# Routed experts with at most 32 tokens: from a block of 128 rows each to four column groups of one shared block

## The chip, the cores and the metric

The kernel runs on one core of one Trainium2 chip. The metric is the device time of one execution in microseconds, taken as the median of the runs of a kernel. The core has five engines with queues of their own: PE (TensorE, matrix products into PSUM; the weight loads are listed as PEld), DVE (VectorE), ACT (ScalarE), POOL (GpSimd) and SP, which here only issues DMA transfers. Each works through its own instructions in order and waits on semaphores for the others.

## The reference

Three stages follow one another: attention with rotary embedding, a sparse mixture of experts (each token goes to one of 8 experts), and a dense one (each token goes through all 8). The change is in the second:

```
logits = xn @ en.T / tau                      # 1152 tokens, 8 experts
expert_idx = np.argmax(logits, axis=1)
gate_w = probs[np.arange(N), expert_idx]
for e in range(E):
    mask = expert_idx == e
    h = np.maximum(x[mask] @ w1[e], 0.0)      # 512 -> 1024
    out[mask] = gate_w[mask, None] * (h @ w2[e])   # 1024 -> 512
```

How many tokens an expert gets is known only when the kernel runs. Worked out on the host from the reference with the inputs it draws, the eight experts get 83, 414, 6, 601, 17, 3, 28 and 0 tokens.

## The kernel before, in words

After attention, `route_half` finds each token's expert, its rank among that expert's tokens, and its place in a list of blocks; a block has 128 rows (`BLK`) of one expert, and an expert takes as many blocks as its tokens need, so 1 + 4 + 1 + 5 + 1 + 1 + 1 + 0 = 14 here. `place` turns the places into an index list per block with small bf16 products on PE, `blocks` writes the expert of each block into `bei`, from which SP loads registers. `NS` blocks (14) are always run, unrolled; a part under `tc.If` (two more blocks) runs only if there are more than `NS`.

One pass of the loop in `run_blocks` is a step `i`, and its instructions are issued in the order in which they are written (a manual schedule fixes it for PE, DVE, ACT and POOL). A step has, on PE: the first layer of block i (`block_l1`, 24 products of 128x512), the transposes of block i+1's tokens (`block_x`), the second layer of block i-1 (`block_l2`, 24 products), and the transposes of block i's hidden layer (`block_turn`). Every fp32 operand is split into a high and a low part of a faster type (fp32r) and three products are summed, so for each block ACT makes a rounded copy of the weights (`whi`, four pieces, L682) and DVE the rest (`wlo`, four pieces, L675). SP fetches the weights of a block only if its expert differs from the block's before. POOL gathers a block's tokens (L690) and scatters its output (L747) by indirect DMA. PSUM has eight banks: four for the first layer (two tiles `h`), two `x` for all transposes and index products, two `y` for the second layer.

At step 1 `place_rest` places the gate values and the scatter indices. In steps 7 to 12 the generator `dense` prepares the first weights of the third stage, whose tiles `w` are a ring of eight in the pool `early`. The third stage (`dense_experts`) follows the blocks; its `sinkhorn` computes routing logits with products of 32 columns in four column groups side by side (L1092), in plain fp32.

Of the kernel before, what the change touches and what calls it, by code (L numbers as in the profile page):

```python
# [25 lines left out]
QT = 120  # L26
TW = [120, 120, 120, 120, 96]
NQ = 5
BLK = 128
NB = 16  # L30
NS = 14
# [9 lines left out]
for name_, width_ in (("u", 128), ("slot", 1), ("rev", E), ("revm", NQ * E), ("j", E * (E + 1)),  # L41
                      ("tri", E * E), ("iota", 128), ("idh", B * NQ), ("idl", B * NQ)):
    COLS[name_] = slice(C_END, C_END + width_)
    C_END += width_
# [3 lines left out]
def fused_kernel(ctx, tc, qk, vv, tab, cst, emb, tau, w1a, w2a, wg, w1b, w2b, out):  # L48
# [22 lines left out]
    gate = keep.tile([BLK, NB], F32, name="gate")  # L71
    idx = keep.tile([BLK, 2, NB], U32, name="idx")
    bei = keep.tile([1, NB + 1], I32, name="bei")
# [319 lines left out]
    mx, fi, rk = tmp("mx", [QT, B, NQ]), tmp("fi", [QT, NQ]), tmp("rk", [QT, NQ])  # L393
# [4 lines left out]
    t9, t8 = tmp("t9", [QT, E, E + 1]), tmp("t8", [QT, E, E])  # L398
    nb, st, en = (tmp(n, [QT, E]) for n in ("nb", "st", "en"))
# [3 lines left out]
    G.memset(ohb[:, :, NQ], 0.0)  # L403

    def route_half(b):
# [16 lines left out]
        if b > 0:  # L422
            V.tensor_tensor(t9, over(rp[:, NQ], 2, [QT, E, E + 1]), col("j", a=E), op=ALU.is_gt)
        yield V.tensor_tensor(w5, rp[:, :NQ], ohb[:, b, :NQ], op=ALU.mult)
        if b > 0:
            V.reduce_sum(out=nb, in_=t9, axis=AX.X)
        yield V.reduce_sum(out=rk, in_=w5, axis=AX.X)
        if b > 0:
            V.tensor_tensor(t8, over(nb, 1, [QT, E, E]), col("tri", a=E), op=ALU.mult)
        yield V.tensor_copy(ri_, rk)  # L430
        if b > 0:
            V.reduce_sum(out=st, in_=t8, axis=AX.X)
# [24 lines left out]
        V.tensor_copy(idx[:, 0], p[:, :NB])  # L457
# [10 lines left out]
    def blocks():  # L468

        be, lim, tx, sx = tmp("be", [1, NB]), tmp("lim", [1, NB]), tmp("tx", [1, NB, E]), [1, NB, E]  # L470
        V.tensor_tensor(en, st, nb, op=ALU.add)
        V.tensor_copy(bei[:, NB:], en[0:1, E - 1:E])
# [4 lines left out]
        V.tensor_copy(bei[:, :NB], be)  # L477

# [6 lines left out]
    gv = tmp("gv", [QT, 3, B, NQ, NB], BF16)  # L485

    def gates():
# [15 lines left out]
        for x in range(3):  # L503
            part = tmp(f"gp{x}", [QT, B * NQ], BF16)
# [7 lines left out]
    def place_rest(bank_):  # L512
# [3 lines left out]
        V.tensor_copy(gate, p[:, :NB])  # L516
# [3 lines left out]
        V.tensor_tensor(ig, idx[:, 0], ig, op=ALU.subtract)  # L520
        V.tensor_copy(idx[:, 1], ig)
# [182 lines left out]
    def block_l1(x, w):  # L704
        p = bank("h", 2, "h", (128, 2, 512))
# [49 lines left out]

    def run_blocks(lo, hi, xb=None, w1=None, w2=None):
# [11 lines left out]
        with tc.manual_schedule(engines=ORDERED):  # L768
# [10 lines left out]
            for i in range(lo, hi + 1):  # L779
                begin, here, more = i == 0, i < hi, i + 1 < hi  # L780

                if here:
                    p = block_l1(x, w1)
                if begin:
# [14 lines left out]
                if begin:  # L799
# [4 lines left out]
                    next(gated)  # L804
                if i + 2 < hi and len(xb) < i + 3 - lo:
# [10 lines left out]
                if i == 1:  # L816
                    place_rest(lambda: bank("x", 2, "gp"))
# [571 lines left out]
```

## Time and profile before

| | us |
|---|---|
| median of 3 runs (lowest, highest) | 1148.04 (1146.05, 1149.77) |
| the profiled execution, device time | 1145.97 |
| its span, first to last instruction | 1144.2 |
| first product of block 0's first layer | 183.9 |
| first transposes of the dense stage | 371.0 |

All times below are of the profiled execution, in us from the start of its span. A row of the timeline gives the start, the time taken, engine, line and operation, the tile written and the tiles read, and how many instructions were merged; the brackets hold the idle time before it and what ended it. Products overlap: the time taken of one is longer than the distance to the next.

### The profile page before, as it was taken

How to read it: one execution, taken by the hardware profiler on the slowest of the kernel's cores; microseconds unless marked ns; L12 is line 12 of the kernel's file. 1: busy time of each engine (PE TensorE's matmuls, PEld its weight loads, DVE VectorE, ACT ScalarE, POOL GpSimd, SP SyncE). 2: the span in 40 equal slices, each digit the busy share in tenths (PEclk: the TensorE clock that was granted, in tenths of full speed). 3: DMA queues.
4: the chain of work that ended last, by engine and by line, in shares of the span. 5: the costliest groups of instructions: out<-in, count | busy, mean ns of one | idle time of the engine just before them, and what ended most of it. 6: DMA issues, size and time to landing. Idle time of an engine off the chain costs nothing.

```text
span 1144.2 us, 17210 instructions
## 1 busy us (share of the span) xinstructions
PE 1120.3 (98%) x6696; PEld 963.3 (84%) x6696; DVE 814.8 (71%) x1262; ACT 507.5 (44%) x772; POOL 145.2 (13%) x109
## 2 busy tenths in 40 slices
PE   8999997999999999999999999999999999999998
PEld 4677775888887998898998899899999899989997
DVE  6767769888884588776667767676667666676665
ACT  4656646888883453333333323333333323332330
POOL 7664402234321000000000000000000000000000
PEclk9999998999999999999999999999999999999999
DMA  8688614273495311111112211111111111111002
GB/s 249 171 238 248 169 32 142 92 256 120 157 340 166 94 38 38 47 47 55 38 38 56 56 38 37 39 55 56 38 38 56 47 46 38 38 56 56 19 1 83
DMA packets 75459, 103.64 MB, mean 91 GB/s; under 512 B 5224, under 2 KB 46696, under 8 KB 74608
## 3 DMA queue, kind: packets, MB, share of 16 engines
q1 hardware_dynamic: 72528, 94.12, 26.8%
q0 software_dynamic: 2240, 7.34, 1.9%
q8 instruction: 53, 0.87, 0.3%
q10 hardware_dynamic: 608, 1.07, 0.2%
q14 instruction: 30, 0.25, 0.1%
HBM read 111.09 MB, written 8.39 MB: 104 GB/s over the span
## 4 chain that ended last, share of the span: by engine, by line
PE 66%; DVE 1%; DMA 1%; issue 0%; POOLq 0%; SPq 0%
PE o L1202 34%; PE d L1148 28%; PE d L1165 2%; DMA g<-yd 0%; DMA yd<-y,idx 0%; DVE acc L1208 0%; PE d L1045 0%; PE o L1092 0%; PE d L1042 0%; DVE h L1190 0%; DVE w L915 0%; DVE w L977 0%; PE o L1045 0%; DVE acc L1213 0%; DVE P L1127 0%
## 5 line engine op out<-in xcount | busy, mean ns | idle before, releaser
L1202 PE MATMUL o<-w,h 128*128 128x512 f32 x1728 | 433.3, 393 | 0.4 <-DVE acc L1208 0.4
L1148 PEld LDWEIGHTS d<-yq,w 128*128 128x128 f32 x2520 | 355.8, 188 | 17.3
L1148 PE MATMUL d<-yq,w 128*128 128x288 f32 x2520 | 367.2, 294 | 0.0
L1202 PEld LDWEIGHTS o<-w,h 128*128 128x128 f32 x1728 | 312.2, 188 | 55.8 <-DVE acc L1208 0.7
L1213 DVE SCALAR_TENSOR_TENSOR acc<-o,P,acc 128x512 f32<-128x512 f32 x252 | 189.1, 750 | 159.0 <-PE o L1202 159.0
L1189 ACT ACTIVATE h<-st 128x576 fp32r<-128x576 f32 x90 | 61.9, 687 | 217.1 <-DVE st L1179 217.1
L1176 ACT ACTIVATE st<-d 128x576 f32<-128x576 f32 x90 | 58.7, 653 | 216.7 <-PE d L1148 216.7
L675 DVE TENSOR_TENSOR wlo<-raw,whi 128x2048 fp32r<-128x2048 f32 x56 | 127.9, 2288 | 17.2 <-ACT whi L682 17.2
L682 ACT ACTIVATE whi<-raw 128x2048 fp32r<-128x2048 f32 x52 | 99.8, 1919 | 9.7 <-DMA raw<-w1a 4.0
L1179 DVE TENSOR_TENSOR st<-st,d 128x576 f32<-128x576 f32 x90 | 67.6, 752 | 39.4 <-PE d L1148 39.4
L247 DVE TENSOR_REDUCE nb<-s 120x1 f32<-120x576 f32 (+1 forms) x80 | 60.3, 754 | 38.7 <-PE s L241 25.3
L253 ACT ACTIVATE p<-s,nb 120x576 f32<-120x576 f32 (+1 forms) x80 | 59.1, 739 | 48.1 <-DVE nb L247 45.8
L914 ACT ACTIVATE w<-raw 128x512 fp32r<-128x512 f32 x124 | 71.4, 576 | 19.8 <-DVE raw L960 16.2
L915 DVE TENSOR_TENSOR w<-raw,w 128x512 fp32r<-128x512 f32 x124 | 76.8, 620 | 0.0
L1190 DVE SCALAR_TENSOR_TENSOR h<-st,h 128x576 fp32r<-128x576 f32 x90 | 67.5, 750 | 0.4 <-ACT h L1189 0.3
L241 PE MATMUL s<-kd,qd 128*120 128x288 f32 x280 | 54.6, 317 | 2.5 <-ACT p L253 2.5
L241 PEld LDWEIGHTS s<-kd,qd 128*120 128x120 f32 x280 | 38.6, 178 | 15.2 <-ACT ph L279 5.7
L298 PE MATMUL o<-ph,vr 120*64 120x288 f32 x320 | 46.8, 417 | 0.0
L740 PE MATMUL y<-whi,hh 128*128 128x512 f32 x112 | 45.0, 402 | 0.0
L740 PE MATMUL y<-wlo,hh 128*128 128x512 f32 x112 | 42.9, 391 | 0.2 <-DVE wlo L675 0.2
L1190 DVE SCALAR_TENSOR_TENSOR h<-d,h 128x576 fp32r<-128x576 f32 x38 | 28.8, 757 | 19.3 <-ACT h L1189 19.3
L747 POOL DMA_INDIRECT yd<-y,idx x14 | 26.8, 1914 | 122.4 <-ACT y L746 97.3
(258 smaller groups left out, 1164.0 us busy)
## 6 DMA issues: line engine op xcount, KB each, us to landing
raw<-w1a SPq DMA_DIRECT2D x56, 512.0 KB
raw<-w2a SPq DMA_DIRECT2D x56, 512.0 KB
raw<-w1b SPq DMA_DIRECT2D x64, 256.0 KB
raw<-w2b SPq DMA_DIRECT2D x32, 512.0 KB
kd<-hl SPq DMA_DIRECT2D x28, 288.0 KB
r<-qk SPq DMA_DIRECT2D x6, 1152.0 KB
qd<-hl SPq DMA_DIRECT2D x28, 144.0 KB
g<-yd SPq DMA_DIRECT2D x4, 576.0 KB
```

What stands on the lines that cost most here:

```text
L241: T.matmul(s[:m, h, :HS], qd[:, j, t * QT:t * QT + m], kd[:, j, x, h * HS:(h + 1) * HS], start=(x == 0), stop=(x == 1))
L675: V.tensor_tensor(lo, raw, hi, op=ALU.subtract)
L682: A.activation(hi, raw, AF.Copy)
L740: T.matmul(p, h[a][:, k * 128:(k + 1) * 128], w[k // 2][b][:, (k % 2) * 512:(k % 2 + 1) * 512], start=(n == 0), stop=(n == len(todo) - 1))
L914: A.activation(hi, src, Copy)
L915: V.tensor_tensor(lo, src, hi, op=ALU.subtract)
L1148: T.matmul(d[1][:, q, :QW], wv[:, wx, which, k], yq[yx][:, YQ[p], k, q * QW:(q + 1) * QW], start=new and k == 0 and (wx, yx) == (0, 0), st ...
L1179: V.tensor_tensor(halves(st[x]), halves(st[x]), mid(d), op=ALU.add)
L1189: A.activation(hi, src, AF.Relu)
L1190: V.scalar_tensor_tensor(lo, src, 0.0, hi, op0=ALU.max, op1=ALU.subtract)
L1202: T.matmul(d, hs[n][:, r, hx, t * 128:(t + 1) * 128], w2[n][:, wx, r], start=(r == 0 and (hx, wx) == (0, 0)), stop=(r == 1 and hx == 1))
L1213: V.scalar_tensor_tensor(a, d, p, a, op0=ALU.mult, op1=ALU.add)
```

## The change

Experts with 1 to 32 tokens, the first four of them (all but expert 0), get no block. They share one further block ("quad") in which group g, rows 32 g to 32 g + 31, belongs to the g-th of them. `NS` becomes 10. The quad's products are plain fp32, without the split: 4 groups x 16 products of 128x32 weights against 128x512, one eighth (`quad_product(s)`, 8 products) at the end of the second layer in steps 2 to 8, the last in step 9. Its tokens are placed in step 1 (`place_quad`), gathered, transposed in step 2 (`quad_tokens`); its ReLU stands in step 5, its hidden layer's transposes in step 6 (`quad_turn`). Its weights are fetched in eight stages of four 512 KB transfers (`quad_fetch`) into the ring of `early`, which it now shares with the dense stage. The first layer has one `h` tile in PSUM where it had two; the two banks become `q`. The steps of `dense` move to 6, 7, 8, 8, 9, 9.

```
-NS = 14
+NS = 10
+NG = 4
+GS = BLK // NG
...
+    def before(dst, src):
+        V.tensor_tensor(t8, over(src, 1, [QT, E, E]), col("tri", a=E), op=ALU.mult)
+        V.reduce_sum(out=dst, in_=t8, axis=AX.X)
...  # in route_half, second half
+            V.tensor_tensor(few, t9[:, :, 0], t9[:, :, E + 1], op=ALU.subtract)
+            V.reduce_sum(out=nb, in_=t9[:, :, :E + 1], axis=AX.X)
+            before(grp, few)
...
+            V.scalar_tensor_tensor(inq, grp, NG - 0.5, few, op0=ALU.is_lt, op1=ALU.mult)
...
+            V.tensor_tensor(nb, nb, inq, op=ALU.subtract)
+            before(st, nb)
+            V.tensor_tensor(en, st, nb, op=ALU.add)
+            V.scalar_tensor_tensor(st, inq, float(NB), st, op0=ALU.mult, op1=ALU.add)
...  # blocks(): five more DVE operations for the experts of the quad
+    def place_quad(bank_):
+        z, qi = tmp("z", [QT, E]), tmp("qi", [BLK, 2])
+        V.tensor_scalar(z, grp, float(GS), 1024.0, op0=ALU.mult, op1=ALU.add)
+        V.scalar_tensor_tensor(z, inq, -1024.0, z, op0=ALU.mult, op1=ALU.add)
+        V.tensor_tensor(ws, ohb[:, :, :NQ], z..., op=ALU.mult)
+        V.tensor_reduce(blk, ws, axis=AX.X, op=ALU.add)
+        V.tensor_tensor(blk, blk, rk, op=ALU.add)
+        V.tensor_tensor(slot..., over(col("iota"), 1, sl), over(blk..., 2, sl), op=ALU.is_equal)
+        p = bank_()
+        for b in range(B):
+            for c in range(NQ):
+                T.matmul(p[:, :6], slot[:m, b, c], qv[:m, n], ...)
...  # then six small DVE operations: idx and gate of the quad
+    def quad_product(s):
+        for n in range(2):
+            k = s if s < KD_ else 2 * (s - KD_) + n
+            if s == 0 or (s, n) == (KD_, 0):
+                quad["p", n] = bank("q", 2, "q")
+            p = quad["p", n if s < KD_ else 0]
+            for g in range(NG):
+                own = slice(g * GS, (g + 1) * GS)
+                T.matmul(p[own], quad["x"][:, k * 128 + g * GS:k * 128 + (g + 1) * GS],
+                         quad["w", s][g][:, n * 512:(n + 1) * 512], ...)
...  # in run_blocks
                 if here:
                     p = block_l1(x, w1)
+                if lo == 0 and i == 2:
+                    quad_tokens()
+                elif lo == 0 and i == 6:
+                    quad_turn()
+                elif lo == 0 and i == 9:
+                    quad_product(7)
+                    block_out(NB, quad["p", 0])
...
                 if i == 1:
                     place_rest(lambda: bank("x", 2, "gp"))
+                    place_quad(lambda: bank("x", 2, "gp"))
+                    quad["xb"] = block_in(NB)
+                if lo == 0 and 2 <= i <= 8:
+                    quad_product(i - 2)
+                    if i == 5:
+                        quad_relu()
...
+                if lo == 0 and 1 <= i <= 7:
+                    quad_fetch(i)
```

DVE in the second half of the routing, from the counts of the experts (`t`, made from `rp`) to the first use of the block starts (`ws`). Before:

```order
L423 TENSOR_TENSOR t_131<-rp,cs 120x72
L424 TENSOR_TENSOR w_126<-rp,ohb 120x40
L426 TENSOR_REDUCE nb<-t_131 120x8
L427 TENSOR_REDUCE rk<-w_126 120x5
L429 TENSOR_TENSOR t_132<-nb,cs 120x64
L430 CAST ri__127<-rk 120x5
L432 TENSOR_REDUCE st<-t_132 120x8
L433 TENSOR_SCALAR rb__128<-ri__127 120x5
L434 TENSOR_SCALAR ri__127<-ri__127 120x5
L445 TENSOR_TENSOR ws<-ohb,st 120x80
```

Now, the first twelve of the seventeen up to `ws`:

```order
L429 TENSOR_TENSOR t_131<-rp,cs 120x80
L430 TENSOR_TENSOR w_126<-rp,ohb 120x40
L432 TENSOR_TENSOR few<-t_131 120x8
L433 TENSOR_REDUCE nb<-t_131 120x8
L408 TENSOR_TENSOR t_132<-few,cs 120x64
L409 TENSOR_REDUCE grp<-t_132 120x8
L435 TENSOR_REDUCE rk<-w_126 120x5
L437 SCALAR_TENSOR_TENSOR inq<-grp,few 120x8
L438 CAST ri__127<-rk 120x5
L440 TENSOR_TENSOR nb<-nb,inq 120x8
L408 TENSOR_TENSOR t_132<-nb,cs 120x64
L409 TENSOR_REDUCE st<-t_132 120x8
```

The expert counts now pass through `few` and `grp` before the block starts `st` exist.

DVE in step 1, where the index products end (`idx<-ig`) and the split of block 1's second-layer weights begins. Before, the split follows at once:

```order
L516 COPY gate<-gp 128x16
L519 TENSOR_SCALAR ig<-gp,cs 128x16
L520 TENSOR_TENSOR ig<-idx,ig 128x16
L521 CAST idx<-ig 128x16
L675 TENSOR_TENSOR wlo<-raw_79,whi 128x2048
```

Now there are six operations up to `slot`, then those that wait for PE's ten products with it (`gp`):

```order
L539 CAST idx<-ig 128x16
L549 TENSOR_SCALAR z<-grp 120x8
L550 SCALAR_TENSOR_TENSOR z<-inq,z 120x8
L551 TENSOR_TENSOR ws<-ohb,z 120x80
L552 TENSOR_REDUCE blk<-ws 120x10
L553 TENSOR_TENSOR blk<-blk,rk 120x10
L555 TENSOR_TENSOR slot<-cs,blk 120x1280
L562 TENSOR_REDUCE qi<-gp 128x1
L563 CAST idx<-qi 128x1
L564 TENSOR_REDUCE gate<-gp 128x1
L565 TENSOR_SCALAR qi<-gp,cs 128x1
L566 TENSOR_TENSOR qi<-qi 128x1
```

On PE the ten products stand between `place_rest` and the transposes of block 1's hidden layer.

ACT in the changed kernel, end of step 5 and start of step 6 (`xh` belongs to block 6's tokens, `raw_79` and `raw_80` are block 5's second-layer weights):

```order
L746 ACTIVATE xh<-xt 128x512
L844 ACTIVATE h<-q 128x512 x2
L728 ACTIVATE whi<-raw_79 128x2048
L792 ACTIVATE y<-y,gate 128x512
L728 ACTIVATE whi<-raw_80 128x2048
L773 ACTIVATE hh<-ht 128x512 x2
L852 ACTIVATE qh<-qht 128x512 x2
L728 ACTIVATE whi<-raw_77 128x2048
```

In the other steps `whi<-raw_79` follows `xh` directly; here the quad's ReLU, which waits for the quad's product behind the second layer, stands between.

## Rows read from the trace of the kernel before

**Rows 1.** The page, part 1: busy us, share of the span, instructions

```profile
PE 1120.3 (98%) x6696; PEld 963.3 (84%) x6696; DVE 814.8 (71%) x1262; ACT 507.5 (44%) x772; POOL 145.2 (13%) x109
```

**Rows 2.** Windows, four steps: stretch, length, busy us per engine, PE clock, DMA, GB/s

```profile
232.30:281.40 49.10, 49.10 (x242) 40.84 (x241) 43.07 (x29) 42.06 (x37) 17.61 (x8) 1.00 0.56 195
```

**Rows 3.** Timeline of PE, one step of the block loop, then the last

```profile
281.49 0.71 PE L710 MATMUL h<-whi,xh 128*128 128x512 f32 x2
...
287.06 0.60 PE L697 MATMUL xt<-io,xb 128*128 128x128 f32 x4
...
293.00 1.03 PE L725 MATMUL ht<-io,h 128*128 128x128 f32 x8
293.79 0.71 PE L710 MATMUL h<-whi,xh 128*128 128x512 f32 x2
...
343.36 0.66 PE L725 MATMUL ht<-io,h 128*128 128x128 f32 x4 [0.59 <-DVE xl L701]
```

**Rows 4.** L1092: the chain's piece, the line's products, timeline of PEld

```profile
384.21 2.75 PE o L1092 x35
...
L1092 PE MATMUL o<-yt,lw x52: 219/379/510, 384.1 to 386.6; 128*32 128x256 f32 x24, 128*32 128x64 f32 x12, 128*32 128x384 f32 x8, 128*32 128x192 f32 x8
...
384.14 1.10 PEld L1092 LDWEIGHTS o<-yt,lw 128*32 128x32 f32 x23 [0.16 <-issue]
...
386.88 1.22 PEld L1165 LDWEIGHTS d<-yq,w 128*128 128x128 f32 x9 [0.41 <-issue]
```

**Rows 5.** Timelines of DVE in the routing, and of PE in step 0

```profile
173.73 0.22 DVE L423 TENSOR_TENSOR t<-rp,cs 120x72 f32<-120x72 f32 x1
...
174.92 0.23 DVE L445 TENSOR_TENSOR ws<-ohb,st 120x80 f32<-120x80 bf16 x1
...
193.44 0.66 PE L725 MATMUL ht<-io,h 128*128 128x128 f32 x4 [1.08 <-DVE xl L701]
```

**Rows 6.** Timelines of PE and DVE in step 1, and line L438

```profile
205.33 0.91 PE L465 MATMUL gp<-gv,slot 120*128 120x16 bf16 x30
206.62 0.40 PE L465 MATMUL gp<-ib,slot 120*128 120x16 bf16 x10 [0.38 <-DVE xl L701]
...
207.53 0.17 DVE L521 CAST idx<-ig 128x16 uint32<-128x16 f32 x1
207.64 4.50 DVE L675 TENSOR_TENSOR wlo<-raw,whi 128x2048 fp32r<-128x2048 f32 x2
...
L438 DVE TENSOR_TENSOR slot<-cs,ri__127 x2: 811/816/820, 151.0 to 176.5; 120x640 bf16<-120x640 f32 x2
```

**Rows 7.** Windows around light stretches of PE, and PE's timeline

```profile
174.90:181.70 6.80, 4.55 (x28) 3.25 (x28) 5.96 (x18) 6.22 (x10) 2.51 (x2) 0.50 0.25 70
181.70:189.50 7.80, 7.13 (x32) 5.44 (x32) 7.31 (x17) 2.52 (x2) 5.29 (x3) 1.00 0.88 316
189.50:193.80 4.30, 1.62 (x12) 1.14 (x11) 3.91 (x9) 3.66 (x5) 0.00 (x0) 1.00 0.26 102
205.30:207.70 2.40, 2.02 (x48) 1.85 (x48) 1.92 (x7) 1.02 (x2) 0.00 (x0) 1.00 0.03 9
...
178.17 3.73 PE L754 MATMUL warm<-whi 128*128 128x512 f32 x8 [0.36 <-DVE en L471]
```

**Rows 8.** Timelines of PE, ACT and DVE from the end of step 2

```profile
219.24 1.03 PE L725 MATMUL ht<-io,h 128*128 128x128 f32 x8
...
219.43 0.69 ACT L746 ACTIVATE y<-y,gate 128x512 f32<-128x512 f32 x1 [0.80 <-PE y L740]
220.02 1.91 ACT L682 ACTIVATE whi<-raw 128x2048 fp32r<-128x2048 f32 x1
221.83 0.58 ACT L727 ACTIVATE hh<-ht 128x512 fp32r<-128x512 f32 x1
...
221.96 2.29 DVE L675 TENSOR_TENSOR wlo<-raw,whi 128x2048 fp32r<-128x2048 f32 x1 [0.50 <-ACT whi L682]
224.17 1.28 DVE L728 TENSOR_TENSOR hl__2498<-ht,hh 128x512 fp32r<-128x512 f32 x2
```

More of the change, by code (lines that the diff above doesn't have):

```diff
@@ L754, in warm, with quad_fetch @@
             T.matmul(p, w[:, :128], w[:, 512:], start=True, stop=True)
+    quad = {}
+    def quad_fetch(s):
+        if not quad:
+            quad["reg"] = [nc.sync.value_load(bei[0:1, NB + 1 + g:NB + 2 + g], min_val=0, max_val=E - 1)
+                           for g in range(NG)]
+        quad["w", s] = []
+        for r in quad["reg"]:
+            w = early.tile([128, F], F32, tag="w", bufs=8, name="qw")
+            ei = bass.ds(r, 1)
+            if s < KD_:
+                nc.sync.dma_start(out=w, in_=w1a[ei, s * 128:(s + 1) * 128, :].rearrange("o p c -> p (o c)"))
+            else:
+                rows_ = slice((s - KD_) * 256, (s - KD_ + 1) * 256)
+                nc.sync.dma_start(out=w.rearrange("p (u c) -> p u c", u=2),
+                                  in_=w2a[ei, rows_, :].rearrange("o (u p) c -> p (o u) c", p=128))
+            quad["w", s].append(w)
@@ new lines, in quad_tokens @@
+    def quad_tokens():
+        pt = bank("x", 2, "qxt")
+        for k in range(KD_):
+            T.transpose(pt[:, k * 128:(k + 1) * 128], quad["xb"][:, k * 128:(k + 1) * 128], ident)
+        quad["x"] = mp.tile([128, F], F32, tag="qx", bufs=1, name="qx")
+        A.activation(quad["x"][:, :DM], pt, AF.Copy)
+    def quad_product(s):
[7 more added lines that the diff above has]
+                T.matmul(p[own], quad["x"][:, k * 128 + g * GS:k * 128 + (g + 1) * GS],
+                         quad["w", s][g][:, n * 512:(n + 1) * 512],
+                         start=(k == 0), stop=(k == (KD_ if s < KD_ else KF) - 1))
@@ new lines, in quad_relu, with quad_turn @@
+    def quad_relu():
+        h = quad["h"] = mp.tile([128, F], F32, tag="h", bufs=2, name="h")
+        for n in range(2):
+            A.activation(h[:, n * 512:(n + 1) * 512], quad["p", n], AF.Relu)
+    def quad_turn():
+        t = mp.tile([128, F], F32, tag="qx", bufs=1, name="qh")
+        for n in range(2):
+            pt = bank("x", 2, "qht")
+            for k in range(4):
+                T.transpose(pt[:, k * 128:(k + 1) * 128], quad["h"][:, (4 * n + k) * 128:(4 * n + k + 1) * 128], ident)
+            A.activation(t[:, n * 512:(n + 1) * 512], pt, AF.Copy)
+        quad["x"] = t
@@ L848, in fused_kernel @@
         banks(mctx, "pm")
-        dense = dense_experts(ctx, tc, yd, wgk, w1b, w2b, out, ident, ones)
+        ctx.enter_context(tc.tile_pool(name="pad", bufs=1, side="right")).tile([128, 8], F32, name="pad")
+        early = ctx.enter_context(tc.tile_pool(name="early", bufs=1, side="right", reuse_waits="tile"))
+        dense = dense_experts(ctx, tc, early, yd, wgk, w1b, w2b, out, ident, ones)
         run_blocks(0, NS, xb, pieces(first_w1), first_w2)
-    with tc.If(nc.values_load(bei[0:1, NB:], min_val=0, max_val=NB) > NS):
+    with tc.If(nc.values_load(bei[0:1, NB:NB + 1], min_val=0, max_val=NB) > NS):
         run_blocks(NS, NB)
@@ L867, in dense_experts @@
     Copy = AF.Copy
-    ctx.enter_context(tc.tile_pool(name="pad", bufs=1, side="right")).tile([128, 8], F32, name="pad")
-    early = ctx.enter_context(tc.tile_pool(name="early", bufs=1, side="right", reuse_waits="tile"))
     free = [0, 1, 2, 3]
```

74 lines of the change are left out of this document (49 added, 25 removed).

## The prediction

> **What bounds the kernel now.** I read the page's first part, then windows of the block loop, then timelines of PE, DVE and ACT around the places that the change touches. The page shows PE busy 98% of the span [rows 1]. That alone would not make every removed product a gain, so the reader looks at the stage: over four steps of the block loop (49.1 us) PE is busy for all of it, DVE 43.1 and ACT 42.1 [rows 2]. A step lasts 293.79 - 281.49 = 12.30 us: 5.6 for the first layer, 5.9 with the four token transposes for the second, 0.8 for the eight hidden transposes [rows 3]. DVE is at 88% of a step, so a step without PE work would not be much shorter than 11 us, but a step taken out whole takes its DVE and ACT work along.
>
> **What goes.** Four steps out of fourteen: 4 x 12.30 = 49.2 us, all on PE's path. The kernel runs ten blocks, as 10 are needed for the drawn token counts (1 + 4 + 5). Besides, PE waited 0.59 us for DVE's `xl` near the end [rows 3], where an expert of one block follows another and the first weights of the dense stage are split too. At the end of the new order one expert has five blocks and each step has more PE work, so I let that go as well: -49.8.
>
> **What comes, on PE's path.**
>
> *Start.* From the counts to the first use of the block starts DVE has nine intervals in 174.92 - 173.73 = 1.19 us, 0.13 each, because independent operations alternate [rows 5]. Now there are sixteen, and most need the one before, so that each costs about its own duration, 0.2 us: some 2.5 us, 1.3 more. PE, the gather of the tokens and all that follow wait for it. `blocks` gets five more (1.0 us) and loses `en` (0.15), ahead of the split of the first weights. In step 0 DVE is the engine waited for: PE's second transposes waited 1.08 us for `xl` [rows 5], and DVE worked without a break to there. So 1.3 + 0.85 = 2.1 us. Bounds: 1.0 (only the routing part, if the rest finds slack) to 3.2.
>
> *Placing the quad.* In step 1 DVE writes the last index at 207.53 and starts the next split at 207.64 [rows 6]. Now five small operations (about 0.2 each) and `slot` come first; 120x640 took 0.816 us [rows 6], twice as wide 1.63. So `slot` is there at 207.64 + 1.1 + 1.63 = 210.4, PE's ten index products take 0.4 as the ten of `place_rest` did [rows 6], and the transposes that began right behind those (206.6 + 0.3) begin at 210.8: 3.9 us. Behind the waiting products on PE are just these transposes and block 2's first layer, so nothing hides it. The second four transposes take over the quad's index bank once four small DVE reads of it are done: 0.7 more. Together 4.6, bounds 3 and 6. The DVE backlog of some 5 us is worked off during steps 2 and 3, whose second layers need their split weights 6 us later.
>
> *The clock.* The granted clock was 0.50 (1.2 GHz) from 174.9 to 181.7, though it was 1.00 in the light stretch 189.5 to 193.8 [rows 7]. The fall came in a stretch without long products that ended at 178.17 [rows 7], and it outlasted it by 3.5 us. The new gap in step 1 is light from 205.3 [rows 6] to about 212.3 (206.6 + 0.3 + 4.6 and 0.8 of transposes), which is longer than the one that kept its clock. I expect a fall there, with 3.5 us of first layer at half speed: 1.8 us lost. Bounds 0 and 3.6.
>
> *Quad products.* No product of exactly this kind is in the trace, but L1092 is close: plain fp32, 32 columns of weights, four groups in turn. Its 26 products appear as 52, two each [rows 4]. Three groups have 1536 columns in sum (4 x 384, or 6 x 256), the fourth 1152: 5760 in all. The stage took 2.75 us [rows 4]. For 1536 columns that is 1.79 ns each, four cycles of 2.4 GHz (1.67) and a remainder; at four cycles, 5760 columns one after another would be 9.6 us and one group alone 2.56. So the groups ran side by side, and 0.19 is left over. A `quad_product` has 2 x 512 columns per group: 1024 x 4 / 2.4 GHz = 1.71 us. To get in and out, PE's weight loads lie idle for 0.16 and 0.41 us [rows 4]; between the 0.19 and the 0.57 I take 0.39: 2.1 us, eight times = 16.8. Bounds 15.2 and 18.2.
>
> The page "TensorE: Matmul & The Clock Gate" of the Trainium skill (Part 3, The mechanism) says that products start and end strictly in program order, only weight loads being pulled ahead. If the two halves of a product stand next to each other, the second half must wait for the first, and the next group behind it. By that, L1092 would take 5760 columns x 2 passes / 2.4 GHz = 4.8 us, and the trace's 2.75 [rows 4] disagrees. For the quad it would be the second case below.
>
> *Transposes and banks.* Step 2 adds four transposes (0.4) in the first layer's wake; they need an `x` bank that DVE, late after the placing, has just read: I put 0.5 on it, 0.9 together (bounds 0.4 and 1.4). In step 6 the eight (0.8) wait longer. Usually ACT copies `whi<-raw_79` while PE runs the second layer; in step 5 the quad's ReLU stands ahead of it, and that waits for the product behind the second layer. Counting from T, the start of the hidden transposes (219.24 in rows 8): two ReLU halves to T+1.3, `whi` 1.9, `y` 0.6, `whi` 1.9 to T+5.7, `wlo` 2.3 to T+8.0, the first `hl` to T+8.6, each by its duration in [rows 8]. In the kernel before, that `hl` starts at 224.17, T+4.9 and is over before the bank is needed. PE comes to the quad's transposes at T+0.8+5.5 = T+6.3, so it waits 2.3 for the first bank, 0.3 for the second, and the token transposes behind wait 0.3 for ACT to empty the first. 0.8 + 2.9 = 3.7, bounds 0.8 and 4.5. The light stretch, about 4 us, is like the 4.3 us from 189.5 that kept the clock [rows 7].
>
> *Hidden.* The single `h` tile: block i's ReLU is over before its transposes, which come ahead of the next first layer anyway. The weights: the same experts are fetched in total, four of them now as 2.1 MB per step. The loop moved 195 GB/s over four steps, 316 at its best [rows 2, 7]; a stage takes 6.6 us at the latter, 10.8 at the former, and has two steps, 28 us. On SP the four transfers wait for a ring tile that PE frees in the same step, and what is behind them is not needed before the next. ACT's few copies outside step 5 fit its idle time (42.1 of 49.1 us busy, [rows 2]). The conditional part grows from two blocks to six and is jumped over as before. Two `dense` steps at once in steps 8 and 9 cost DVE 1.3 us in steps that now last 14.
>
> **The sum.** -49.8 + 2.1 + 4.6 + 1.8 + 16.8 + 0.9 + 3.7 = -19.9. From the profiled 1145.97 that is 1126.1. The profiled execution lies at the lower end of the three runs (1146.05 to 1149.77) and 2.1 below their median; the changed kernel's runs will scatter likewise, so I add half: 1127. With all bounds on one side the sum is -29 to -12, which so many unknowns hardly do together; 1117 to 1134 is this case's own range.
>
> **The rivals.**
>
> Second case, *groups half in step*: the two halves of each product hold up the next group. 16 sets x 4 x 512 x 2 / 2.4 GHz = 27.3 us instead of 13.7, so 1127 + 13.6 = 1141. For it: a product is two instructions [rows 4]. Against: the 2.75 us.
>
> Third, *weights late*: between steps 2 and 5 four quad stages and the next expert's 4.2 MB come together, 12.6 MB. At 195 GB/s that takes 65 us, against 4 x 14.4 = 58 us of steps: 7 late, 1134. For it: 195 GB/s is what the loop moved. Against: nothing asked for more there, and 316 was reached.
>
> Fourth, on the other side, *one after another*: the four groups take turns on PE, each product with its full 0.85 us. 64 x 0.85 = 54.6 instead of 13.7, 40.9 more: 1168, slower than before. It decides from 2.5 times the side-by-side time on, (13.7 + 20) / 13.7. For it: the quad streams four different weight tiles of 512 columns, twice what most of L1092's products have. Against: L1092 streams different data per group as well.
>
> Fifth, *the change does not do what it says*: more than ten blocks, so that the conditional part runs its six, 6 x 12.3 = 74 us and a reload: 1200. For it only that the counts are data; worked out from the reference they give exactly ten.
>
> **Chances.** Forecast 0.78, second 0.06, third 0.10, fourth 0.04, fifth 0.01, and 0.01 for something between the third and the fourth that ends near the time before. A measurement of this kernel tells 0.3%, about 3.4 us, from no change. The first three are faster: 0.94; the fourth and fifth slower: 0.05; within 0.3%: 0.01. The range 1114 to 1138 takes in the forecast's own and the third case.
>
> **What would show it.** L1092's analogue (the quad's eight calls) at 2.1 us each, the groups' products starting together: if a call is 3.8 or 7, the second or fourth case holds. Step to step 14.4 us for steps 3, 4 and 7, more in step 6, where PE's `qht` waits for DVE `hl` or ACT. In step 1 PE idle some 3.5 us before the products `gp<-qv`, released by DVE `slot`, and a window of 0.50 behind it. Block 0's first layer starts some 1.3 us behind 183.9, block 1's by 2.1. Wrong would be: PE waiting for `qw` transfers, a step without extra wait of 13 us or less, or DVE as releaser in every step.

## The result and the profile after

The changed kernel's median is 1129.31 us (1128.28 to 1130.21, four runs), that of the kernel before, run beside it, 1148.9 (1146.05 to 1150.91, four runs). The ratio is 0.983, with an interval of 0.981 to 0.986. The forecast was 1127, so the time came out 2.3 above it and inside both ranges. The profiled execution took 1128.46 with a span of 1126.7, which is 17.5 less span than before; the sum had said 19.9. The mechanism was right, but the difference hides two terms of the sum that were missing and some others that were too large, so that the total lies nearer to the forecast than its parts do.

The page's first part of the kernel after (busy us, share of the span, instructions; against [rows 1]):

```profile
PE 1097.5 (97%) x6606; PEld 930.1 (83%) x6606; DVE 777.4 (69%) x1257; ACT 467.8 (42%) x742; POOL 131.6 (12%) x106
```

PE gave up 22.8 us of work and the span 17.5: some 5 us of idle time are new. Windows of the kernel after find them and the clock's part (stretch, length, busy us and instructions of PE, PEld, DVE, ACT and POOL, granted clock, DMA share, GB/s):

```profile
190.40:195.60 5.20, 1.69 (x13) 1.18 (x12) 4.10 (x9) 4.97 (x5) 0.00 (x0) 1.00 0.35 141
196.20:199.60 3.40, 3.40 (x10) 2.62 (x9) 3.40 (x4) 0.69 (x2) 0.00 (x0) 0.50 0.00 0
213.30:216.70 3.40, 3.40 (x22) 2.97 (x21) 2.95 (x7) 1.19 (x2) 1.97 (x1) 0.50 0.03 11
230.50:273.40 42.90, 42.90 (x230) 31.72 (x229) 32.03 (x21) 29.86 (x28) 13.29 (x6) 1.00 0.76 282
343.00:346.40 3.40, 3.40 (x9) 2.62 (x10) 0.00 (x0) 0.00 (x0) 0.07 (x1) 0.50 0.39 134
```

The row from 230.50 is three undisturbed steps: PE busy in all of them, as in [rows 2], but DVE only 75% and ACT 70%, and the DMA at 282 GB/s where it had been 195. Two stretches at 0.50 (1.2 GHz) lie in the block loop, at 196 and 213, and one at its end, at 343. Only the one at 213 was foreseen.

PE's timeline of the kernel after, at the places that the prediction speaks of (start, us, line, tile written from tiles read, instructions; in brackets the idle time before and what ended it):

```profile
213.19 0.42 PE L561 MATMUL gp<-qv,slot 120*128 120x6 bf16 x10 [3.30 <-DVE slot L555]
213.47 1.96 PE L771 MATMUL ht<-io,h 128*128 128x128 f32 x8
...
227.82 1.92 PE L837 MATMUL q<-qw,qx 128*32 128x512 f32 x16
229.68 1.12 PE L771 MATMUL ht<-io,h 128*128 128x128 f32 x8
...
272.59 1.09 PE L771 MATMUL ht<-io,h 128*128 128x128 f32 x8
280.56 1.25 PE L851 MATMUL qht<-io,h 128*128 128x128 f32 x8 [1.40 <-DVE hl__3014 L774]
...
342.86 8.23 PE L1160 MATMUL d<-w 128*128 128x512 f32 x28 [3.26 <-PEq L971]
350.94 1.21 PE L1163 MATMUL d<-io,g 96*128 96x96 f32 x12
```

A quad call starts at 227.82 and what is behind it at 229.68: 1.86. Its sixteen instructions start in four sets of four, those of a set within 0.02 of each other and the sets some 0.43 apart. At 213.19 the quad's index products had waited 3.30 for DVE's `slot`; at 280.56 its hidden transposes waited 1.40 for `hl`. And at 342.86, outside the blocks, PE begins again 3.26 after its last block product, held by its queue's way out of the conditional part (L971).

From the starts of the same products in both traces, the whole difference divides so (us):

| | predicted | measured |
|---|---|---|
| four steps removed | -49.8 | -49.98 |
| start (1.29 before block 0, 1.09 in step 0) | 2.1 | 2.38 |
| placing the quad in step 1 (0.72 of it transposes at 0.50) | 4.6 | 3.9 |
| clock in steps 1 and 2, first layers alone | 1.8 | 2.4 (1.64 + 0.77) |
| quad products, eight calls | 16.8 | 16.2 |
| token transposes in step 2 | 0.9 | 0.42 |
| transposes and waits in step 6 | 3.7 | 2.92 |
| last block product to first dense transposes | 0 | 2.35 |
| dense stage, first transposes to last product | 0 | 2.52 |
| attention, ahead of all that was changed | 0 | -0.62 |
| sum | -19.9 | -17.5 |

The steps last 11.02, 19.46, 15.47, 14.28, 14.30, 14.31, 17.22, 14.30 and 14.31; before, 9.93, 13.91 and then 12.27 to 12.29, the last 13.11.

### The profile page after: what moved, and what is told of

Its sections match the earlier page's. It is cut to its first block, busy times and chain, and to the rows that moved or that the text cites. A ratio compares the mean times of both kernels' runs of the same rounds, so it can differ in the third digit from the quotient of the medians.

```text
span 1126.7 us, 16883 instructions
## 1 busy us (share of the span) xinstructions
PE 1097.5 (97%) x6606; PEld 930.1 (83%) x6606; DVE 777.4 (69%) x1257; ACT 467.8 (42%) x742; POOL 131.6 (12%) x106
## 4 chain that ended last, share of the span: by engine, by line
PE 68%; DVE 1%; issue 0%
PE o L1320 35%; PE d L1266 29%; PE d L1283 2%; PE d L1160 1%; DVE acc L1326 0%; PE d L1163 0%; PE o L1210 0%; DVE h L1308 0%; DVE w L1033 0%; DVE w L1095 0%; PE o L1163 0%; DVE acc L1331 0%; DVE P L1245 0%; DVE rs L1234 0%; PE o L1241 0%
## 5 line engine op out<-in xcount | busy, mean ns | idle before, releaser
L1320 PE MATMUL o<-w,h 128*128 128x512 f32 x1728 | 435.6, 394 | 0.4 <-DVE acc L1326 0.4
L1266 PE MATMUL d<-yq,w 128*128 128x288 f32 x2520 | 367.3, 294 | 0.0
L721 DVE TENSOR_TENSOR wlo<-raw,whi 128x2048 fp32r<-128x2048 f32 x40 | 91.2, 2289 | 29.3 <-ACT whi L728 28.8
L728 ACT ACTIVATE whi<-raw 128x2048 fp32r<-128x2048 f32 x36 | 68.9, 1914 | 17.6 <-PE h L756 11.6
L283 DVE COPY ph<-pt 120x480 f32<-120x480 f32 x64 | 41.3, 647 | 2.2 <-PE pt L277 2.2
L1095 DVE TENSOR_TENSOR w<-raw,w 128x1024 fp32r<-128x1024 f32 x32 | 39.0, 1218 | 0.4 <-ACT w L1094 0.4
L277 PE MATMUL pt<-io,p 120*120 120x120 f32 x256 | 37.0, 267 | 1.2 <-DVE ph L283 1.2
```

What stands on the lines that cost most here:

```text
L721: V.tensor_tensor(lo, raw, hi, op=ALU.subtract)
L728: A.activation(hi, raw, AF.Copy)
L1266: T.matmul(d[1][:, q, :QW], wv[:, wx, which, k], yq[yx][:, YQ[p], k, q * QW:(q + 1) * QW], start=new and k == 0 and (wx, yx) == (0, 0), st ...
L1320: T.matmul(d, hs[n][:, r, hx, t * 128:(t + 1) * 128], w2[n][:, wx, r], start=(r == 0 and (hx, wx) == (0, 0)), stop=(r == 1 and hx == 1))
```

## The experiments

Eleven kernels, each changed from the kernel after. All but the last were run once, so what counts in them is the length of a step or of a stage in the trace, not the total: the first of the address runs below, in which no stage changed by its edit, took 1127.52, 1.8 less than the median of the kernel after.

**Column groups.**

```
-            for g in range(NG):
-                own = slice(g * GS, (g + 1) * GS)
+            for g in range(2 if s in (1, 2) else NG):
+                own = slice(0, GS) if s in (5, 6) else slice(g * GS, (g + 1) * GS)
```

It leaves out groups 2 and 3 in stages 1 and 2, and in stages 5 and 6 sends all four groups to the first one's columns.

> Left out: in quad stages 1 and 2 (steps 3 and 4) the products of groups 2 and 3; in stages 5 and 6 (steps 7 and 8) all four groups write column group 0, so the quad's output is another. Stages 0, 3, 4 and 7 are as in the changed kernel, where a call takes 1.86 us from its first product to the next transposes and a step 14.30 us. Theory (the groups run side by side, and a call lasts as long as one group's columns): with two groups the call keeps its 1.86 us and steps 3 and 4 stay at 14.3. Rival (products take turns, or the weight loads set the pace): two groups take about half, 1.0 us, steps of 13.4. All in one column group: theory 4 x 1.71 = 6.8 us a call, steps 7 and 8 about 19.3 us; rival: no change.

PE's timeline of this run:

```profile
242.85 1.91 PE L837 MATMUL q<-qw,qx 128*32 128x512 f32 x8
244.69 1.09 PE L771 MATMUL ht<-io,h 128*128 128x128 f32 x8
...
302.95 7.05 PE L837 MATMUL q<-qw,qh 128*32 128x512 f32 x16
309.93 1.09 PE L771 MATMUL ht<-io,h 128*128 128x128 f32 x8
```

With half the products a call takes 1.84 (242.85 to 244.69), as with all; in one column group it takes 6.98, and steps 7 and 8 last 19.42 and 19.41 instead of 14.3. There the instructions start one by one, 0.43 apart. So the groups run side by side, and the fourth case would have cost 5.1 more per call. The page "TensorE: Matmul & The Clock Gate" of the Trainium skill (Part 3, Measured speedup vs the span model) gives 2.38 for three column tiles; here four gave 6.98 / 1.86 = 3.75. No run here had three.

**Placing the quad a step later.** The slots are made at the end of step 1, the placing follows in step 2, and the token transposes in step 3; two calls share step 5.

```
-                if lo == 0 and i == 2:
+                if lo == 0 and i == 3:
                     quad_tokens()
...
+                if lo == 0 and i == 2:
                     place_quad(lambda: bank("x", 2, "gp"))
...
-                if lo == 0 and 2 <= i <= 8:
-                    quad_product(i - 2)
+                if lo == 0 and 3 <= i <= 8:
+                    for s in {3: (0,), 4: (1,), 5: (2, 3)}.get(i, (i - 2,)):
+                        quad_product(s)
...
+                if i == 1:
+                    slot_quad()
...
-                    quad_fetch(i)
+                    for s in {1: (1,), 2: (), 3: (2,), 4: (3,), 5: (4, 5)}.get(i, (i,)):
+                        quad_fetch(s)
```

> The quad is placed a step later and off PE's path: DVE makes the slots at the end of step 1, PE's ten index products stand behind the second layer in step 2, the token transposes in step 3, the eight products in steps 3, 4, 5, 5, 6, 7, 8, 9. Theory (PE stood still 3.3 us in step 1 for DVE's slots, and the light stretch lowered the clock in step 2): the wait goes, the fall at 213 goes, steps 1 and 2 together some 3.3 + 0.8 us shorter, up to 1 us given back to DVE's backlog in steps 2 and 3: 3 to 4 us in all. Rival (the step is held by DVE's own work, so the slots only move the wait): PE waits in step 2 or 3 for xl or hl instead and the whole gains under 1.5 us.

The steps: 9.72, 15.24, 14.12, 15.06, 14.28, 16.75, 20.16, 14.28, 14.31. Step 1 became 4.2 shorter, and none of the falls at 196 and 213 came in this run (the one in the routing, ahead of the blocks, lasted longer instead, from 173.9 to 187.6); but the first block product to the last took 153.85 against 154.61, 0.8 less, and the whole run 1129.54, no less than the kernel after. The 0.8 is as small as the rival had it, for another reason. Steps 1 and 2 are 5.6 shorter, of which 2.4 are work that now stands later; step 0, which the edit does not touch, is 1.3 shorter too; and step 6 took 2.9 more than in the kernel after. PE's timeline and its waits there, and SP's:

```profile
284.60 1.05 PE L841 MATMUL q<-qw,qh 128*32 128x512 f32 x4
286.31 1.04 PE L841 MATMUL q<-qw,qh 128*32 128x512 f32 x2 [0.66 <-DMA qw<-w2a]
287.67 1.91 PE L841 MATMUL q<-qw,qh 128*32 128x512 f32 x10 [0.31 <-DMA qw<-w2a]
289.50 1.09 PE L775 MATMUL ht<-io,h 128*128 128x128 f32 x8
```

```profile
274.20 2.88 SPq L84 DMA_DIRECT2D raw<-w2a  x4
277.35 5.65 SPq L821 DMA_DIRECT2D qw<-w2a  x8
```

The call takes 4.90 instead of 1.86, because its weights were asked for only from 277.35 on, in its own step. The two calls of step 5 had freed the ring tiles by 269.4, but in SP's order this fetch stands behind that of block 6's second layer, which waited until 274.20 for DVE's `wlo` to free a tile of its own. So the stall in step 1 is real and can be removed, and the prediction's third case (weights late) is real as well once a fetch has less than a step.

**The quad's ReLU behind the split.** Moved from behind the products of step 5 to behind the hidden transposes (`block_turn`).

```
-                    if i == 5:
-                        quad_relu()
...
+                if lo == 0 and i == 5:
+                    quad_relu()
```

> The quad's ReLU on ACT stands behind the hidden transposes of step 5, no longer ahead of the split of block 5's second-layer weights. Theory (ACT's queue behind the ReLU made hl late, and with it the transpose banks of step 6): step 6 falls from 17.2 us to 15.1 (14.3 plus the eight transposes), 2.1 us in all. Rival (the transposes wait for the ReLU itself or for emptying the banks): step 6 stays above 16.5.

PE's timeline of this run:

```profile
278.07 1.04 PE L851 MATMUL qht<-io,h 128*128 128x128 f32 x8
279.36 0.66 PE L743 MATMUL xt<-io,xb 128*128 128x128 f32 x4 [0.25 <-ACT qh L852]
```

The wait for `hl` is gone; step 6 takes 15.64 instead of 17.22. Of the 2.92 by which the transposes and waits lengthened step 6, 1.6 were thus the ReLU's place in ACT's queue, where 2.1 had been expected; 0.25 of the rest is the wait for ACT to empty the bank. The run took 1126.68, its span 1124.5.

**A conditional part of two blocks.** Enough only for these token counts, since the part is not run.

```
-        run_blocks(NS, NB)
+        run_blocks(NS, NS + 2)
```

> The conditional part holds two blocks (rows for block 10 and 11) where it held six; it isn't entered. Theory (jumping over the longer part costs an instruction refetch: SP's first instruction behind the jump came 4.2 us after it, PE's branch took 3.5): from the last second-layer product to the first dense transposes 9.4 us as in the kernel before, 2.3 less than the 11.7 of the changed kernel. Rival (SP comes late because its last weight transfer for the dense stage was issued late, at 339.6): stays at 11 or more.

PE's timeline of this run:

```profile
340.92 6.64 PE L1160 MATMUL d<-w 128*128 128x512 f32 x28 [1.17 <-ACTq L971]
349.75 2.18 PE L1163 MATMUL d<-io,g 96*128 96x96 f32 x12 [2.19 <-DMA g<-yd]
```

PE's branch out of the conditional part took 0.35 instead of 3.55, the warming products ran at full clock (6.64, not 8.23), yet the stretch to the dense transposes shrank only from 11.74 to 10.40: now they wait 2.19 for the transfer of `g`. A second chain ends there. The dense stage gave part of it back, as the clock fell in its first microseconds (349.7 to 353.1), and the run took 1129.08.

**The dense preparation off step 9.** The last two pieces of `dense` go ahead of the last quad call, so that SP's queue is through earlier.

```
                 elif lo == 0 and i == 9:
+                    next(dense)
+                    next(dense)
                     quad_product(7)
...
-                if lo == 0 and i in (6, 7, 8, 9):
+                if lo == 0 and i in (6, 7, 8):
```

> The two preparation steps of the dense stage that stood at the end of step 9 stand ahead of the quad's last product in step 9; the conditional part keeps its six blocks. Theory (SP reached the jump 2.2 us after the last second-layer product because the dense weights' last transfers waited for that preparation, and the jump's 4.2 us came on top): SP jumps before the last product, and the tail to the dense transposes falls from 11.7 to about 9.4 us although PE's own branch still takes 3.5. Rival (PE's branch sets the tail): it stays above 11.

PE's timeline of this run:

```profile
342.25 8.24 PE L1162 MATMUL d<-w 128*128 128x512 f32 x28 [3.52 <-PEq L973]
350.33 1.15 PE L1165 MATMUL d<-io,g 96*128 96x96 f32 x12
```

SP issued the load of `g` 5.66 after the last block product instead of 7.20, and the dense transposes came no earlier (12.0). By itself this edit is worth nothing that can be told: PE's own way through the branch and the warming products ends last. The theory that SP alone was the cause fell here.

**Both edits of the tail.** The two edits above in one kernel.

```
+                    next(dense)
+                    next(dense)
                     quad_product(7)
...
-        run_blocks(NS, NB)
+        run_blocks(NS, NS + 2)
```

> The edits of two earlier runs together: the conditional part holds two blocks where it held six, and the dense preparation of step 9 stands ahead of the quad's last product. Alone they left the tail from the last second-layer product to the dense transposes at 10.4 and 12.0 us, against 11.7. Theory (two chains end there, SP's late arrival and PE's branch of 3.5 us with the 28 warming products behind it at the lower clock; taking one away leaves the other): 9.4 us, as before the change. Rival (the two don't add, the scatter of the last rows sets the rest): 10.4 or more.

PE's timeline of this run:

```profile
340.52 6.64 PE L1162 MATMUL d<-w 128*128 128x512 f32 x28 [1.17 <-ACTq L973]
348.34 1.21 PE L1165 MATMUL d<-io,g 96*128 96x96 f32 x12 [1.18 <-DMA g<-yd]
```

The stretch is 9.38 long, as before the change (9.39). So the 2.35 come from two chains that end within about a microsecond of each other: PE's branch with the warming products, and SP's branch with the load of `g`. Either edit alone leaves the other chain. The run took 1126.46, its span 1124.5. That the two lengths agree to 0.01 is luck, as the same tail scatters: in the eight runs that keep the kernel after's, itself among them, the stretch took 11.74 to 13.64. Both runs with the short part lie below all of these; the 12.00 of the dense preparation alone lies among them. PE's branch is steadier: 3.49 to 3.94 in the ten runs with six blocks, 0.353 in the three with two.

**Products that keep the clock up.** Ten warming products in step 0, behind block 1's token transposes, and fourteen between `place_rest` and `place_quad`.

```
                     x = block_x(xb[1])
+                    warm(w1[0][0], 10)
...
                     place_rest(lambda: bank("x", 2, "gp"))
+                    warm(w2[0][0], 14)
                     place_quad(lambda: bank("x", 2, "gp"))
```

> Idle stretches filled with products whose result isn't used: 10 of 128x512 in step 0 while PE waits for block 0's ReLU, 14 in step 1 ahead of the quad's index products. Theory (the clock fell at 196 and at 213 because of light stretches of PE): no window of 0.50 between 185 and 330, block 1's first layer 5.34 us (6.95 before), block 2's 5.34 (6.09), about 2.4 us less up to step 3. Rival (the falls have nothing to do with the light stretches): both stay.

A window over both places in this run:

```profile
185.00:230.00 45.00, 42.61 (x255) 33.00 (x254) 38.14 (x65) 26.90 (x25) 11.32 (x9) 1.00 0.58 217
```

The granted clock is 1.00 throughout, the first layers of blocks 1 and 2 take 5.32 and 5.34 instead of 6.95 and 6.09, and the way from block 0's first layer to step 3 is 44.33 instead of 45.95. That is 1.6 of the 2.4 booked to the clock: step 2 gained 0.75 of its 0.77, step 1 gained 1.24 of its 1.64, and step 0 became 0.37 longer. The eight other runs that share the code of these steps took 44.8 to 46.6 on this way, so one run does not settle the 1.6; that the two falls were absent is what the window shows.

**Where the dense stage's 2.52 come from.** Its line that takes the most time, line groups of before and of after (busy us, mean ns, idle time before):

```profile
L1202 PE MATMUL o<-w,h 128*128 128x512 f32 x1728 | 433.3, 393 | 0.4 <-DVE acc L1208 0.4
```

```profile
L1320 PE MATMUL o<-w,h 128*128 128x512 f32 x1728 | 435.6, 394 | 0.4 <-DVE acc L1326 0.4
```

The same 1728 products take 2.3 us more, with the same waits and, from 373 on, a granted clock of 1.00 in both: each is 1.3 ns slower. Three runs look for what made them so. The first allocates two tiles of 4 KB per partition ahead of the weight ring in the pool `early`:

```
+        for _ in range(2):
+            early.tile([128, KD_, 2, 128], F32, tag="raw1", bufs=2, name="raw1")
         dense = dense_experts(ctx, tc, early, yd, wgk, w1b, w2b, out, ident, ones)
```

> Only addresses change: the dense stage's raw tiles again lie ahead of the ring of weight tiles in the pool, as in the kernel before; nothing is added to any queue. Theory (the dense stage's products have grown slower by where its tiles lie, 1.4 ns each of 1728): the dense stage, first transposes to last product, falls from 771.3 to 768.7 us as before. Rival (the shift of 64 bytes of all other tiles does it, or neither): stays at 771.3.

771.23 us for the stage, as after (771.26). The order within the pool is not it. The second widens a small tile kept below the pool, so that everything above it moves by 64 bytes per partition:

```
-    keep.tile([128, 8], F32, name="pad")
+    keep.tile([128, 24], F32, name="pad")
```

> Only addresses change: 64 bytes of padding per partition more in front of the dense stage's own tiles (128 in all against the kernel before, so that they lie at an odd multiple of 64 again); the ring stays where the changed kernel has it. Theory of the run before (the ring's place): the dense stage stays at 771.3 us. Rival (the shift by 64): back to 768.7.

772.80, slower still: neither the 771.3 nor the 768.7 that were expected. The other large line of the stage now moved too (367.3 in the kernel after):

```profile
L1266 PE MATMUL d<-yq,w 128*128 128x288 f32 x2520 | 368.9, 295 | 0.0
```

The whole run was at 1134.65 (span 1132.8); it lost time in attention too, where the clock fell at 125.7, so its total says nothing on this. The third lays `gate` and `idx` in one tile and drops the small one, so that the pool starts where it did before the change:

```
-    gate = keep.tile([BLK, NB + 1], F32, name="gate")
-    idx = keep.tile([BLK, 2, NB + 1], U32, name="idx")
+    both = keep.tile([BLK, 3 * (NB + 1)], F32, name="both")
+    gate = both[:, :NB + 1]
+    idx = both[:, NB + 1:].bitcast(U32).rearrange("p (x n) -> p x n", x=2)
...
-    keep.tile([128, 8], F32, name="pad")
```

> Only addresses change: the gate and index tiles share one tile and a padding tile goes, so that every tile of the dense stage's own pool lies where it lay in the kernel before (64 bytes lower than in the changed kernel); the ring of weight tiles stays where the changed kernel has it. Theory (the products of the dense stage slow down with the place of that pool: 768.7 us in the kernel before, 771.3 with 64 bytes more, 772.8 with 128 more): the dense stage takes 768.7 us. Rival (something in the changed program ahead of it, not the place): stays at 771.3.

```profile
L1320 PE MATMUL o<-w,h 128*128 128x512 f32 x1728 | 433.4, 393 | 0.4 <-DVE acc L1326 0.4
```

The line is back, and the stage takes 768.79 as before the change (768.74). By the sizes of the tiles, each rounded up to 32 bytes, the pool starts at byte 17984 of a partition in this run and before, at 18048 after, at 18112 in the second run: 768.8, 771.3, 772.8. The line took 433.3 or 433.4 in the three runs with the pool at the first place and 435.6 or 435.7 in all nine at the second. So the address decides. Why these should be slower no run shows.

**All together.** The quad placed late, with the products of stages 0 and 1 both in step 3, so that stages 3 and 4 are fetched a step earlier than in the late placing above, the ReLU late, the dense preparation off step 9, eight warming products in step 0, 18 instead of 28 ahead of the dense stage, and the third run's addresses. The conditional part keeps its six blocks, so that any token counts are served.

```
...
-                    quad_product(i - 2)
...
+                    for s in {3: (0, 1)}.get(i, (i - 2,)):
+                        quad_product(s)
...
-                    quad_fetch(i)
+                    for s in {1: (1,), 2: (), 3: (2, 3)}.get(i, (i,)):
+                        quad_fetch(s)
...
```

> All that the runs point to, with the conditional part kept at six blocks: slots at the end of step 1, index products in step 2, token transposes in step 3, products 0 and 1 in step 3 and then one a step (so that no stage's weights are asked for early), the ReLU behind the hidden transposes of step 5, eight warming products in step 0, the dense preparation of step 9 earlier, 18 warming products in front of the dense stage where there were 28, and the dense stage's tiles where they lay before the change. Against the changed kernel (profiled span 1126.7): 3 us from the placing and its clock fall, 1.5 from the ReLU, 1.0 from the warming in step 0, 1.3 from the tail, 2.5 from the addresses: some 9 us, span about 1117.5, 0.975 of the kernel before. Rival (weights of stage 2 come late in step 4, or DVE's backlog takes the placing's gain): 1120 to 1122.

The median is 1122.28 (1121.26 to 1125.15, five runs) beside 1147.37 of the kernel before (1146.31 to 1149.76): a ratio of 0.978 (0.977 to 0.980), whose interval lies below that of the kernel after. The span is 1120.3, some 3 more than expected and in the rival's band, though no wait for the quad's weights came. Of the parts, steps 0 to 3 gained 2.67, step 6 1.63, the tail 1.25 (10.49) and the dense stage 2.50 (768.76); attention ended 1.68 later, which the edits don't touch. What is short of the expectation is this 1.68 and some 1.3 in steps 0 to 3. Step 0's warming products, eight where the run with the warming products alone had ten, did not hold the clock this time, and the branch still costs PE 3.29:

```profile
197.10:200.60 3.50, 3.36 (x10) 2.88 (x11) 3.04 (x4) 1.59 (x3) 0.00 (x0) 0.51 0.00 0
```

```profile
239.45 3.64 PE L841 MATMUL q<-qw,qx 128*32 128x512 f32 x32
...
340.22 5.94 PE L1172 MATMUL d<-w 128*128 128x512 f32 x18 [3.29 <-PEq L983]
```

Two calls in a row take no wait for weights (32 products in 3.64), so the schedule cures what the late placing alone brought up.

## Why the prediction was right, and where it was not

*What bounds the kernel, and the four steps.* Right: PE was the bound of a step and a removed one gave its full length, 49.98. The bounds of the sum, given as -29 to -12, add up to -29.4 and -12.9, which leaves the range as it was.

*Quad products.* Right in mechanism and size: 1.86 in the call and 2.01 in a step that has one, for 2.1. The reading of L1092 [rows 4] was sound; the first experiment shows the two-group and the one-column case beside it. The second and fourth cases are excluded.

*The start.* 2.38 for 2.1, half of it by luck. The 1.29 ahead of block 0 is what was described: DVE's stretch from the counts to the first use of the block starts ([rows 5]: 1.19) takes 2.47, for 2.5. The 1.09 in step 0 was to come from DVE's five operations more. But in this execution ACT stood still until 190.31 for the transfer of block 1's first weights, where before it was 187.56, and the ReLU that PE's transposes wait for stands behind that copy (2.64 of waiting, before 1.60). ACT's timeline before, then after:

```profile
187.56 1.92 ACT L682 ACTIVATE whi<-raw 128x2048 fp32r<-128x2048 f32 x1 [3.69 <-DMA raw<-w1a]
```

```profile
190.31 1.91 ACT L728 ACTIVATE whi<-raw 128x2048 fp32r<-128x2048 f32 x1 [5.77 <-DMA raw<-w1a]
```

In seven other runs that share this step the weights came sooner, DVE worked without a break, and step 0 took 10.23 to 10.83 where it had been 9.93: 0.3 to 0.9 more, for 0.85. Why the transfer landed late here no run shows. DVE's rows of the start, then of step 1:

```profile
173.11 0.23 DVE L429 TENSOR_TENSOR t<-rp,cs 120x80 f32<-120x80 f32 x1
...
175.58 0.23 DVE L456 TENSOR_TENSOR ws<-ohb,st 120x80 f32<-120x80 bf16 x1
...
210.41 0.18 DVE L539 CAST idx<-ig 128x16 uint32<-128x16 f32 x1
...
211.64 1.49 DVE L555 TENSOR_TENSOR slot<-cs,blk 120x1280 bf16<-120x1280 f32 x1
```

*Placing the quad.* The chain was as described: five small operations from 210.41 to 211.64 (1.23 for 1.1), `slot` in 1.49 for 1.63, then the products, with nothing on PE to hide it. The 3.9 are PE's 3.30 of waiting, 0.28 for the products and 0.72 because the eight transposes ran at 0.50 (1.60 from their start to the first layer's, before 0.88), less the 0.38 that PE had waited there before [rows 6]. So the placing itself cost 3.2 for 4.6. The 0.7 for the bank's reads was too much: at the low clock they are over before the second four transposes, and with the clock held, in the run with the warming products, those began some 0.4 late.

*The clock.* The fall behind the gap in step 1 was foreseen and came, for 3.4 us. It came in all nine runs that keep this gap, beginning between 210.07 and 215.02, and in none of the three in which the gap is filled or gone (the warming products, the late placing, all together); so this part is shown. It cost block 2's first layer 0.77 and the transposes ahead of it the 0.72 above. What failed is that nothing was put down for the end of step 0: the clock fell there too, at 196.2, for another 1.64. With the transposes the clock took 3.1, for 1.8. In this execution the late weights had made that light stretch longer, 5.2 us from 190.40 where [rows 7] have 4.3, but that this brought the fall is not shown: of the ten runs that share step 0 five had it and five did not, and windows over the stretch, in the run with the ReLU moved (where the clock fell at 195.0) and in the one with the dense preparation moved (where it did not), are alike:

```profile
190.20:195.00 4.80, 1.84 (x14) 1.33 (x13) 4.63 (x10) 4.38 (x6) 0.00 (x0) 1.00 0.31 125
```

```profile
190.40:195.20 4.80, 1.86 (x15) 1.31 (x13) 4.62 (x10) 4.31 (x6) 0.00 (x0) 1.00 0.30 124
```

In the nine runs the first layers of blocks 1 and 2 lost 1.6 to 3.3 together, so no forecast of this term can come closer than that.

*Step 6.* Right in its chain: ACT's ReLU waits for the product, and `whi`, `wlo` and `hl` are late behind it. T, the start of the hidden transposes, is 272.59 here. ACT's and DVE's timelines:

```profile
271.94 0.60 ACT L844 ACTIVATE h<-q 128x512 f32<-128x512 f32 x1 [3.72 <-PE q L837]
...
273.30 1.91 ACT L728 ACTIVATE whi<-raw 128x2048 fp32r<-128x2048 f32 x1
...
275.67 1.91 ACT L728 ACTIVATE whi<-raw 128x2048 fp32r<-128x2048 f32 x1
277.47 1.08 ACT L773 ACTIVATE hh<-ht 128x512 fp32r<-128x512 f32 x2
```

```profile
275.24 4.67 DVE L721 TENSOR_TENSOR wlo<-raw,whi 128x2048 fp32r<-128x2048 f32 x2 [4.57 <-ACT whi L728]
279.82 1.28 DVE L774 TENSOR_TENSOR hl__3014<-ht,hh 128x512 fp32r<-128x512 f32 x2
```

The first half of the ReLU started 0.65 ahead of T, as its bank's products are done half a call earlier; so `hl` began at T+7.2 and not at some T+8, and PE waited 1.40 where 2.3 were predicted.

*Weights.* The third case did not happen: no wait for `qw` in the kernel after, at 282 GB/s. It is nearer than the chance of 0.10 sounds, since one fetch that came late in SP's order made it true.

*Hidden things.* Here the prediction failed. "The conditional part grows from two blocks to six and is jumped over as before" was put at nothing without a row for its price. It cost 2.35: PE's branch takes 3.55 instead of 0.35, SP issues `g` 7.20 after the last block product instead of 4.29, and behind the pause the warming products ran at half clock from 343.0 to 346.4. PE's branch before and after, then PE's and SP's timelines before and SP's after (PE's stands above):

```profile
L851 PEldq COMPARE_BRANCH  x1: 353/353/353, 361.4 to 361.4; - x1
```

```profile
L971 PEldq COMPARE_BRANCH  x1: 3549/3549/3549, 339.0 to 339.0; - x1
```

```profile
362.86 6.64 PE L1042 MATMUL d<-w 128*128 128x512 f32 x28 [0.89 <-ACTq L851]
370.98 1.21 PE L1045 MATMUL d<-io,g 96*128 96x96 f32 x12 [1.48 <-DMA g<-yd]
```

```profile
365.88 2.89 SPq L1033 DMA_DIRECT2D g<-yd  x4
```

```profile
346.40 1.90 SPq L1151 DMA_DIRECT2D g<-yd  x4
```

The two further pieces of `dense` in steps 8 and 9, costed at nothing because DVE has room, were counted on the wrong queue: it is SP that came late by them, and only in the experiments with a short conditional part does it show. The dense stage had no term at all, as the change does not touch it; the tables' new sizes moved its pool, and 1728 of its products became a little slower, 2.3 of the 2.52.

These two add up to 4.87; the other terms, together 2.5 better than predicted, gave half of it back. That they did is luck: 0.6 of the 2.5 is attention's end, ahead of all that was changed, and the rest comes from terms of the table that are each off by less than 1.

## What to carry to other kernels

Small groups of rows that would each fill a tile of their own are worth putting side by side in column groups: four plain fp32 products side by side took here no longer than two, and their block cost 2.0 us in each of eight steps, and some 12 in all for the start, the placing, the clock and the transposes, for four steps of 12.3 saved. When costing such a change, look also at everything that it resizes outside its own stage: the length of a conditional part, the tables whose size sets the addresses of later pools, and the light stretches of PE that it makes. And a wait that ends a stretch may hide a second chain right behind it, so test the edits of a stall together as well as one by one.

## What the runs showed of the hardware

- A shift of 64 bytes in the place of a pool changes the rate of full 128x512 products: 433.3 us for 1728 before, 435.6 shifted, 433.4 with the old place; a second 64 bytes slowed the 128x288 ones as well (367.3 to 368.9).
- Leaving a conditional part that is not run takes longer when it holds more: PE's branch took 0.35 us with two blocks in it (three runs), 3.49 to 3.94 with six (ten runs).
- Four column groups gave 3.75 times the rate of one (1.86 and 6.98 us a call); the halves of the fp32 products did not hold up the next group, as the four groups' instructions start within 0.02 us of each other.
- The same light stretch of PE, 4.8 us with PE busy for 1.84 and 1.86, was followed by a clock of 0.50 in one run and not in another.
